# Local attention of a two-layer mixture kernel cut into units of 32 queries by 128 keys, with the turned probabilities as the stationary side of P V

## The chip, the cores and the metric

The kernel runs on one core of a Trainium2 chip, as one launch. The metric is the time of the device for one execution, in microseconds (us). The core has a matrix engine (TensorE, PE in the rows; its weight loads are PEld), VectorE (DVE), ScalarE (ACT), GpSimd (POOL) and SyncE (SP), which here only issues transfers (DMA).

## The reference, cut to what matters

```python
B, H, Sl, Sg, D = 4, 8, 512, 32, 64
k_all, v_all = concat([k_g, k_l]), concat([v_g, v_l])
out_g = sm(scale * q_g @ k_all.T) @ v_all                  # 32 global queries see all 544 keys
mask = abs(pos[:, None] - pos[None, :]) <= 32              # a local query sees 65 neighbours ...
s_ll = where(mask, scale * q_l @ k_l.T, -1e9)
out_l = sm(concat([scale * q_l @ k_g.T, s_ll])) @ v_all    # ... and the 32 global keys
x = concat([out_g, out_l], axis=2)                         # 4 x 544 = 2176 tokens of 512
h = x @ w_in ; x = (h * clip(h + 3, 0, 6) / 6) @ w_out     # 512 -> 2048 -> 512
out = max(x @ w1, x @ w2, x @ w3) @ w_out2                 # 512 -> 768 -> 512
```

`sm` takes the exponential of the row less its maximum and divides by the sum of the row plus 1e-9.

## The kernel before

**Stages.** Attention goes by batch b (4) and pair of heads pr (4 pairs), 16 pairs in all; the two heads of a pair lie in the two halves of the 128 partitions. Its result X, split into two fp32r parts, feeds the first product (`first`): 960 matmuls, 576 of 512 columns (token chunks 0 to 2) and 384 of 320 columns (chunks 3 and 4). Behind it come the second product in seven Strassen products (line 837), the third in seven (961), and the last (961, 1116).

**What sets the order.** Every step is an `op` with an engine, an estimated time and a due time; `Plan.order` puts the steps of each engine into one fixed order when the kernel is built. At run time each engine goes through its own list in that order and waits where a step is not ready. Attention steps are due by `STEPS` (s0 of a pair); `first` has a late due time (1e4 and more), so it fills PE's list where attention leaves room. SP issues nearly all transfers from one list.

**A pair before.** Keys are laid out as global, 256 local, global, 256 local, global (608 columns), so that 128 queries find their keys in a window of 224 columns. `scores` (L449) makes 16 matmuls of 64 queries by 128 to 192 keys with the two heads side by side. `rowmax` (L463, DVE) adds the mask and takes the maximum, `expo` (L469, ACT) the exponential and the sum, `guard` and `recip` (L480 to L485) make one over the sum, `norm` (L494, POOL) multiplies P by it. `flip` (L506) turns P by 16 transposes, four copies (`flipped`, L410) take it out of PSUM, and `pv` (L532) multiplies with V (64 columns) as the stationary side and turned P as the moving side, which leaves the result with the head's 64 values down the partitions, as X wants it (`x_hi` L547, `x_lo` L549).

**Global queries** go for two pairs at a time (`globals_`): `g_scores` (L566), `g_rowmax` (L570), `g_exp` (L578), `g_norm` (L583), five transposes (`g_flip`, L592), `g_pv` (L607), `g_x` (L611).

**Weights of the first product** (16 loads `raw`, 512 KB each) are decoded by DVE, ACT and POOL (L620 to L647) in the same stretch; after `first`, relu and gate (L683, L685) and the sums for Strassen (L655) follow, and the results go to DRAM (`gsA`, `gsB`, `gsC`).

**PSUM.** Five banks `s`, one bank `o` and two banks 6 and 7 serve attention and `first` until `end_of_attention`. There are three buffers each for Q, K and V.

Of the kernel before, what the change touches and what calls it, by code (L numbers as in the profile page):

```python
# [34 lines left out]
KEYS = {(0, 0): (0, 128), (0, 64): (0, 192), (1, 0): (0, 192), (1, 64): (64, 224),  # L35
        (2, 0): (0, 160), (2, 64): (32, 224), (3, 0): (32, 224), (3, 64): (96, 224)}
LOCAL = (((32, 192, 0),), ((0, 160, 96), (192, 32, 256)), ((0, 32, 224), (64, 160, 256)), ((0, 192, 320),))
SEEN = ((((0, 128), (0, 128)), ((1, 96), (64, 128))), (((0, 128), (0, 128)), ((1, 96), (0, 128))),
        (((0, 128), (0, 128)), ((1, 96), (32, 128))), (((1, 96), (0, 128)), ((0, 128), (0, 96))))
# [207 lines left out]
PAIRS = 3  # L247
SPLIT = 2
WIDE = 4
TS = "BC"  # L250
STEPS = (7.2, 13, 13, 15)
LAG = 92.0
# [12 lines left out]
def body(ctx, tc, q_n, k_n, v_r, w_in, w_o, w_3, w_4, out):  # L265
# [65 lines left out]
    mask_t = att.tile([128, 4, WIN], BF16, name="mask", bufs=1)  # L331
    nothing = att.tile([128, 288], BF16, name="nothing", bufs=1)
    mask = [Buf(tile=mask_t[:, 2 * u:2 * u + 2]) for u in range(2)]
    for u in range(2):
        nc.gpsimd.memset(mask_t[:, 2 * u:2 * u + 2], 0.0)
        for i in (2 * u, 2 * u + 1):
            for a, n, k0 in LOCAL[i]:

                far = 128 * i - k0
                for base, step in ((32 - far, 1), (32 + far, -1)):  # L340
                    if base + min(-step * 127, 0) + min(step * (n - 1), 0) < 0:
                        nc.gpsimd.affine_select(
                            out=mask_t[:, i, a:a + n], in_=mask_t[:, i, a:a + n], compare_op=ALU.is_ge, fill=-2.0 ** 33,
                            base=base, pattern=[[step, n]], channel_multiplier=-step)
# [10 lines left out]
    NTB = 8  # L355
    tbufs = []
    for i in range(NTB):
        t = att.tile([128, 2, 256], F32, name=f"tbuf{i}", bufs=1)
        nc.vector.memset(t[:, :, WIN:256], 0.0)
        tbufs.append(t)  # L360
    tg_t = att.tile([128, 640], F32, name="tg", bufs=1)
    nc.vector.memset(tg_t[:, 288:320], 0.0)
    nc.vector.memset(tg_t[:, NK:640], 0.0)
# [12 lines left out]
    T["vr"] = tag("vr", 3, [128, 2, 5, D], F32, "att")  # L376
    T["t"] = Tag("t", NTB, lambda slot: tbufs[slot], "att")
    T["tg"] = Tag("tg", 1, lambda slot: tg_t, "att")
    T["nm"] = tag("nm", 4, [128, 3, 2, 2], F32, "att")
    T["pt"] = tag("pt", 6, [128, 512], F32, "att")  # L380
    T["g1"] = tag("g1", 2, [128, 4], F32, "att")
# [34 lines left out]
    def pair(b, pr, s0):  # L416

        S = {}
        held[b, pr] = S
        Q, K, V = Buf(T["qr"]), Buf(T["kr"]), Buf(T["vr"])  # L420
        S["Q"], S["K"], S["V"] = Q, K, V

        for n, (t, src, cut, size) in enumerate(((Q, q_n, 256, NQ + SG), (K, k_n, 352, NK))):
            for i, (a, z) in enumerate(((0, cut), (cut, size)) if b + pr == 0 else ((0, size),)):
                e, issue = ("ACT", nc.scalar) if b + pr == 0 and n else ("SP", nc.sync)
                op(e, 0.45, lambda t=t, src=src, a=a, z=z, issue=issue: issue.dma_start(
                    out=t()[:, a:z], in_=src[b, pr][:, a:z]), s0 - 6 + i, w=[(t, i)] if b + pr == 0 else [t],
                   kb=(z - a) / 2, rel=s0 - 14, what="qk"[n])
        op("SP", 0.5, lambda: nc.sync.dma_start(out=V(), in_=v_r[b, pr]), s0 - 3 + 5 * (b + pr == 0), w=[V], kb=320, rel=s0 - 10, what="v")

        ob, PTS = Buf(T["o"]), {}

        for grp in (((0, 1),) if b >= PAIRS else ((0,), (1,))):
            SB, TB, NM, PT, FB = {}, {}, {}, {}, {}
            k, s1 = len(grp), s0 + 2 * grp[0]
            for u in grp:
                SB[u], TB[u] = ([Buf(T[x]) for _ in range(2)] for x in ("l" if b == 0 and u and pr < WIDE else "s", "t"))
                NM[u] = Buf(T["nm"])

            def scores(grp=grp, SB=SB):  # L440

                for u in grp:
                    for v in range(2):
                        i = 2 * u + v
                        for m in (0, 64):
                            for hh in range(2):
                                o, bank = 64 * hh, SB[u][hh]
                                a, z = KEYS[i, m]
                                nc.tensor.matmul(bank()[m:m + 64, v * WIN + a:v * WIN + z],  # L449
                                                 lhsT=Q()[o:o + 64, 128 * i + m:128 * i + m + 64],  # L450
                                                 rhs=K()[o:o + 64, 128 * i + a:128 * i + z], start=True, stop=True)

            need = [(Q, grp[0]), *((K, u) for u in range(grp[0] + 1))] if len(grp) == 1 else [Q, K]
            head = op("PE", 0.62 * k, scores, s1, r=need, after=full if b + pr == 0 else (),
               w=[x for u in grp for x in SB[u]] + [(t, "held") for u in grp for t in TB[u]], what="scores")
            if not full[6:]:
                full.append(filled(sbanks[4], [head]))
            for u in grp:
                sb, tb, nm = SB[u], TB[u], NM[u]
                for v in range(2):  # L460
                    for hh in range(2):
                        def rowmax(v=v, hh=hh, i=2 * u + v, sb=sb, tb=tb, nm=nm):
                            nc.vector.tensor_tensor_reduce(  # L463
                                out=tb[hh]()[:, v, 0:WIN], in0=sb[hh]()[:, v * WIN:v * WIN + WIN], in1=mask[i // 2]()[:, i % 2],
                                scale=-0.125, scalar=3.0e38, op0=ALU.add, op1=ALU.min, accum_out=nm()[:, 0, hh, v:v + 1])

                        def expo(v=v, hh=hh, tb=tb, nm=nm):
                            t = tb[hh]()[:, v, 0:WIN]
                            nc.scalar.activation(out=t, in_=t, func=ACTF.Exp, scale=-1.0, bias=nm()[:, 0, hh, v:v + 1],  # L469
                                                 accum_out=nm()[:, 1, hh, v:v + 1])  # L470

                        op("DVE", 0.47, rowmax, s0 + 2 * u + 1 + .2 * v, r=[(sb[hh], v), mask[u]],
                           w=[(tb[hh], v), (nm, (0, v, hh))], what="rowmax")
                        op("ACT", 0.665, expo, s0 + 2 * u + 2.2 + .2 * v, r=[(nm, (0, v, hh))],
                           w=[(tb[hh], v), (nm, (1, v, hh))], what="exp")

                def guard(e, nm=nm):
                    s = nm()[:, 1].rearrange("p h v -> p (h v)")
                    if e == "ACT":
                        nc.scalar.activation(out=s, in_=s, func=ACTF.Identity, bias=tiny)  # L480
                    else:
                        nc.gpsimd.tensor_tensor(out=s, in0=s, in1=tiny.to_broadcast([128, 4]), op=ALU.add)

                def recip(nm=nm):
                    nc.vector.reciprocal(out=nm()[:, 2], in_=nm()[:, 1])  # L485

                sums = [(nm, (1, v, hh)) for v in range(2) for hh in range(2)]
                op(("ACT", "POOL"), (0.295, 0.12), guard, s0 + 2 * u + 3, w=sums, what="guard", two=("POOL",))
                op("DVE", 0.175, recip, s0 + 2 * u + 3.5, r=sums, w=[(nm, 2)], what="recip")
                for hh in range(2):  # L490
                    def norm(hh=hh, tb=tb, nm=nm):
                        t = tb[hh]()[:, :, 0:WIN]
                        r = nm()[:, 2, hh].rearrange("p (v o) -> p v o", o=1).to_broadcast([128, 2, WIN])
                        nc.gpsimd.tensor_tensor(out=t, in0=t, in1=r, op=ALU.mult)  # L494

                    op("POOL", 0.98, norm, s0 + 2 * u + 4, r=[(nm, 2)], w=[(tb[hh], 0), (tb[hh], 1)], what="norm", two=True)
            for u in grp:
                FB[u], PT[u] = ([Buf(T[x]) for _ in range(2)] for x in ("f", "pt"))

            def flip(grp=grp, TB=TB, FB=FB):  # L500
                for u in grp:
                    for hh in range(2):
                        for v in range(2):
# [15 lines left out]
            if ONCE <= b < PAIRS:  # L519
                if not grp[0]:  # L520
                    continue
                grp, k = (0, 1), 2
# [682 lines left out]
```

## Time and profile before

| | |
|---|---|
| median of 3 runs | 733.1 us (731.78 to 734.84) |
| profiled execution, span | 729.2 us |
| the profiled execution's own time beside its span | not listed apart; the median lies 3.9 us over the span |
| PE busy | 717.7 us (98%) |
| DVE, ACT, POOL busy | 535.3, 411.0, 189.8 us |
| moved by DMA | 131.34 MB, mean 180 GB/s |

Busy time of PE counts matmuls that overlap in its pipeline, so it is not the time that the work needs; for that the chain of work that ended last is read, where each group of matmuls has the time from its start to the start of the next group.

### The profile page before, as it was taken

How to read it: one execution, taken by the hardware profiler on the slowest of the kernel's cores; microseconds unless marked ns; L12 is line 12 of the kernel's file. 1: busy time of each engine (PE TensorE's matmuls, PEld its weight loads, DVE VectorE, ACT ScalarE, POOL GpSimd, SP SyncE). 2: the span in 40 equal slices, each digit the busy share in tenths (PEclk: the TensorE clock that was granted, in tenths of full speed). 3: DMA queues.
4: the chain of work that ended last, by engine and by line, in shares of the span. 5: the costliest groups of instructions: out<-in, count | busy, mean ns of one | idle time of the engine just before them, and what ended most of it. 6: DMA issues, size and time to landing. Idle time of an engine off the chain costs nothing.

```text
span 729.2 us, 14100 instructions
## 1 busy us (share of the span) xinstructions
PE 717.7 (98%) x5329; PEld 638.1 (88%) x5329; DVE 535.3 (73%) x1100; ACT 411.0 (56%) x858; POOL 189.8 (26%) x225
## 2 busy tenths in 40 slices
PE   8999999999999999999999999999999999999998
PEld 6777878788888899988898899898999999998998
DVE  6979676546777766589976768999877886485881
ACT  7997889555544444356663457673644334253552
POOL 6685869322203122111000001121210220011210
PEclk9999999999999999999999999999999999999999
DMA  7455775424368884676565669401453562355652
GB/s 279 129 180 193 253 256 192 153 72 165 140 209 295 317 307 171 233 260 195 174 206 156 202 196 312 127 2 32 133 172 134 173 228 69 102 170 198 175 159 88
DMA packets 73140, 131.34 MB, mean 180 GB/s; under 512 B 4976, under 2 KB 43632, under 8 KB 72048
## 3 DMA queue, kind: packets, MB, share of 16 engines
q1 hardware_dynamic: 72784, 130.13, 53.6%
q8 instruction: 42, 0.69, 0.4%
q10 hardware_dynamic: 288, 0.31, 0.1%
q14 instruction: 26, 0.21, 0.1%
HBM read 84.93 MB, written 45.48 MB: 179 GB/s over the span
## 4 chain that ended last, share of the span: by engine, by line
PE 79%; DMA 6%; DVE 5%; ACT 4%; POOL 3%; issue 2%; SPq 0%; ACTq 0%; DVEq 0%; POOLq 0%
PE bank L961 31%; PE bank L673 21%; PE bank L837 20%; PE s L506 2%; ACT tbuf L469 2%; POOL rq L655 2%; PE o L532 2%; PE s L449 1%; DMA raw<-in_w_in_dram 1%; DMA gsA<-rq 1%; DMA kr<-in_kn_dram 1%; PE bank L1116 1%; POOL tbuf L494 1%; DVE rr L655 1%; PE s L607 1%
## 5 line engine op out<-in xcount | busy, mean ns | idle before, releaser
L673 PE MATMUL bank<-rx,rw 128*128 128x512 f32 (+1 forms) x960 | 199.1, 363 | 1.1 <-DVE rq L685 1.1
L673 PEld LDWEIGHTS bank<-rx,rw 128*128 128x128 f32 x960 | 161.2, 188 | 26.8 <-issue 4.3
L837 PE MATMUL bank<-rr,rw 128*128 128x320 f32 (+2 forms) x912 | 155.1, 331 | 1.0 <-DVE rr L655 0.9
L837 PEld LDWEIGHTS bank<-rr,rw 128*128 128x128 f32 x912 | 140.2, 188 | 15.0 <-DVE rr L655 1.9
L961 PE MATMUL bank<-rw,rr 128*128 128x256 f32 (+2 forms) x648 | 99.7, 302 | 1.1 <-DVE rf L973 0.7
L961 PEld LDWEIGHTS bank<-rw,rr 128*128 128x128 f32 x648 | 90.6, 188 | 6.1 <-DVE rf L973 1.1
L760 ACT CAST rr<-fw 128x1024 fp32r<-128x1024 f32 (+2 forms) x76 | 62.1, 820 | 52.3 <-PE bank L837 40.5
L655 DVE TENSOR_TENSOR rr<-fw,rr 128x1024 fp32r<-128x1024 f32 (+2 forms) x76 | 71.7, 947 | 25.1 <-ACT rr L760 24.4
L655 POOL TENSOR_TENSOR rf<-rf 128x256 f32<-128x256 f32 (+2 forms) x35 | 37.5, 1080 | 157.2 <-DVE rf L655 58.8
L469 ACT ACTIVATE tbuf<-tbuf,nm 128x224 f32<-128x224 f32 x128 | 60.6, 479 | 11.0 <-DVE nm L463 10.9
L685 DVE SCALAR_TENSOR_TENSOR rq<-rq,bank 128x512 f32<-128x512 f32 (+1 forms) x60 | 37.1, 619 | 38.4 <-ACT rq L683 38.1
L494 POOL TENSOR_TENSOR tbuf<-tbuf,nm 128x448 f32<-128x448 f32 x64 | 61.0, 973 | 8.4 <-DVE nm L485 4.9
L683 ACT ACTIVATE rq<-bank,three 128x512 f32<-128x512 f32 (+1 forms) x60 | 37.9, 632 | 43.5 <-PE bank L673 40.3
L410 ACT COPY rf<-bank 128x512 f32<-128x512 f32 (+2 forms) x72 | 33.2, 468 | 39.9 <-PE bank L961 29.5
L961 PE MATMUL bank<-rw,re 128*128 128x256 f32 (+2 forms) x369 | 54.2, 292 | 0.7 <-DVE bank L410 0.7
L961 PE MATMUL bank<-re,rr 128*128 128x512 f32 x222 | 54.8, 391 | 0.0
L655 POOL TENSOR_TENSOR rq<-rq 128x256 f32<-128x256 f32 (+2 forms) x45 | 38.5, 861 | 54.1 <-DVE rq L655 49.5
L961 PEld LDWEIGHTS bank<-rw,re 128*128 128x128 f32 x369 | 49.4, 188 | 2.4 <-DVE bank L410 0.9
L961 PEld LDWEIGHTS bank<-re,rr 128*128 128x128 f32 x222 | 40.8, 188 | 8.1
L1055 DVE TENSOR_TENSOR rf<-rf,bank 128x320 f32<-128x320 f32 (+2 forms) x72 | 37.0, 528 | 13.0 <-PE bank L961 11.7
L463 DVE CUSTOM_DVE_ANT_0 tbuf<-s,mask 128x224 f32<-128x224 f32 x112 | 36.9, 383 | 6.7 <-PE s L449 6.4
L506 PE MATMUL s<-ident,tbuf 128*128 128x128 f32 x256 | 33.9, 276 | 0.4 <-POOL tbuf L494 0.2
(131 smaller groups left out, 1047.4 us busy)
## 6 DMA issues: line engine op xcount, KB each, us to landing
fw<-gsB SPq DMA_DIRECT2D x28, 512.0 KB, 4.8
raw<-in_w_dram SPq DMA_DIRECT2D x24, 512.0 KB, 4.3
fw<-gsC SPq DMA_DIRECT2D x28, 320.0 KB, 3.6
raw<-in_w_in_dram SPq DMA_DIRECT2D x16, 512.0 KB, 4.0
raw<-in_w_o_dram SPq DMA_DIRECT2D x16, 512.0 KB, 4.9
fw<-gsA SPq DMA_DIRECT2D x28, 256.0 KB, 2.8
gsB<-rq SPq DMA_DIRECT2D x6, 1024.0 KB, 5.1
rf<-hd SPq DMA_DIRECT2D x14, 384.0 KB, 4.9
```

The source lines that it names most:

```text
L463: nc.vector.tensor_tensor_reduce(out=tb[hh]()[:, v, 0:WIN], in0=sb[hh]()[:, v * WIN:v * WIN + WIN], in1=mask[i // 2]()[:, i % 2], scale=-0 ...
L469: nc.scalar.activation(out=t, in_=t, func=ACTF.Exp, scale=-1.0, bias=nm()[:, 0, hh, v:v + 1], accum_out=nm()[:, 1, hh, v:v + 1])
L494: nc.gpsimd.tensor_tensor(out=t, in0=t, in1=r, op=ALU.mult)
L506: nc.tensor.transpose(FB[u][hh]()[:, at:at + 128], TB[u][hh]()[:, v, kb * 128:kb * 128 + 128], ident)
L655: ENG[e].tensor_tensor(out=out, in0=a, in1=b, op=f)
L673: nc.tensor.matmul(ps()[:, 0:m], lhsT=w[:, i, k], rhs=xs(c)[:, j, k], start=(k == 0 and s == 0), stop=(k == KC - 1 and s == 2))
L683: op("ACT", us, lambda ps=ps, m=m, out=out: nc.scalar.activation(out=out(), in_=ps()[:, 0:m], func=ACTF.Relu, bias=three), -100, r=[ps], w ...
L685: op("DVE", us, lambda ps=ps, m=m, out=out: nc.vector.scalar_tensor_tensor(out=out(), in0=out(), scalar=6.0, in1=ps()[:, 0:m], op0=ALU.min ...
L760: op("ACT", act(n) + 0.01, lambda: nc.scalar.copy(out=out(0), in_=src()), due, r=r, w=[(w, "hi")], what=what + "_hi")
L837: nc.tensor.matmul(A[e]()[:, 0:n], lhsT=w[:, 2 * fp + f, u, e], rhs=r[:, v, f], start=(seed is None and fp + f + s == 0), stop=(fp == 3 an ...
L961: nc.tensor.matmul(bank()[:, 0:n], lhsT=w[:, u, k], rhs=r[:, v, k], start=(start and k + s == 0), stop=(k == K - 1 and s == 2), skip_group ...
L1055: op("DVE", dve(n), lambda q=q, src=src, mv=mv: nc.vector.tensor_tensor(out=mv(q)(), in0=mv(q)(), in1=src(), op=ALU.max), -200, r=[bank], ...
```

## The change

A pair is now cut into 16 units of 32 queries with one window of 128 keys each: the keys are laid out as global, 64 local, global, 64 local, ... (800 columns), and a copy of V in windows of 128 rows is made on the host for each unit (2048 columns in place of 640). `scores` makes 32 matmuls of 32 queries by 128 keys, `rowmax` and `expo` work on 128 columns in place of 224, `flip` makes 8 transposes, and P is not normalized. `pv` has turned P (32 queries) as the stationary side and V (64 columns) as the moving side; its result has the queries down the partitions, is multiplied by one over the sums (`norm`, DVE, 512 columns) and turned by 4 transposes (`xflip`). The global queries follow the same manner. `STEPS` and `LAG` have other values, and the host function lays out K and V.

```diff
-STEPS = (7.2, 13, 13, 15)
-LAG = 92.0
+STEPS = (5.6, 9, 9, 10)
+LAG = 114.0
...
-FORM = dict(scores="Q", pv="H", g_scores="H", g_pv="H")
+FORM = dict(scores="Q", pv="R", g_scores="H", g_pv="R")
...
-    T["vr"] = tag("vr", 3, [128, 2, 5, D], F32, "att")
+    T["vr"] = tag("vr", 3, [128, 2, NW, D], F32, "att")
...
+        op("SP", 0.5, lambda: nc.sync.dma_start(out=V(), in_=v_r[b, pr]), s0 - 3 + 5 * first_, w=[V], kb=1024, rel=s0 - 10, what="v")
...
+                for i in tiles:
+                    for c in range(4):
+                        j = 4 * i + c
+                        a, z = SG * (j == 0), 128 - SG * (j == NW - 1)
+                        for hh in range(2):
+                            nc.tensor.matmul(SB[hh]()[QB * c:QB * c + QB, 128 * i + a:128 * i + z],
+                                             lhsT=Q()[64 * hh:64 * hh + 64, QB * j:QB * j + QB],
+                                             rhs=K()[64 * hh:64 * hh + 64, AT[j] + a:AT[j] + z], start=True, stop=True,
+                                             tile_position=(64 * hh, QB * c))
...
-                    def norm(hh=hh, tb=tb, nm=nm):
-                        t = tb[hh]()[:, :, 0:WIN]
-                        r = nm()[:, 2, hh].rearrange("p (v o) -> p v o", o=1).to_broadcast([128, 2, WIN])
-                        nc.gpsimd.tensor_tensor(out=t, in0=t, in1=r, op=ALU.mult)
...
+            def flip(hh=hh, FB=FB):
+                for i in range(4):
+                    nc.tensor.transpose(FB()[:, 128 * i:128 * i + 128], TB[hh]()[:, i], ident)
...
+            for i in range(4):
                 for hh in range(2):
+                    at = 128 * i + D * hh
+                    for c in range(4):
+                        nc.tensor.matmul(OB()[QB * c:QB * c + QB, at:at + D], lhsT=PT[hh]()[:, 128 * i + QB * c:128 * i + QB * c + QB],
+                                         rhs=V()[:, hh, 4 * i + c], start=True, stop=True, tile_position=(0, QB * c))
...
+        def norm():
+            r = NM()[:, 2].rearrange("p i h -> p (i h)").rearrange("p (x o) -> p x o", o=1).to_broadcast([128, 8, D])
+            nc.vector.tensor_tensor(out=OX().rearrange("p (x d) -> p x d", d=D), in0=OB().rearrange("p (x d) -> p x d", d=D),
+                                    in1=r, op=ALU.mult)
...
+        def xflip():
+            for i in range(4):
+                nc.tensor.transpose(XT()[:, 128 * i:128 * i + 128], OX()[:, 128 * i:128 * i + 128], ident)
...
+            for c, (j, k) in enumerate(GCHUNK):
+                for n, Z in enumerate(R):
                     for hh in range(2):
+                        x = 64 * n + 32 * hh
+                        at = 128 * (c % 4) + x
+                        nc.tensor.matmul(og()[x:x + 32, 0:D], lhsT=pts_g[c // 4]()[0:k, at:at + 32], rhs=Z["V"]()[0:k, hh, j],
+                                         start=(c == 0), stop=(c == 5), tile_position=(0, x))
```

The change moves instructions. On SP, at the start of the program, the list of transfers of before reads as follows (`qr`, `kr` and `vr` are the buffers of Q, K and V, `raw` that of encoded weights; the figures are partitions by elements).

```order
L426 DMA qr<-in_qn_dram 128x576
L426 DMA kr<-in_kn_dram 128x608
L429 DMA vr<-in_v_dram 128x640 x2
L426 DMA qr<-in_qn_dram 128x576
L426 DMA kr<-in_kn_dram 128x608
L642 DMA raw<-in_w_in_dram 128x4x256
L429 DMA vr<-in_v_dram 128x640
L642 DMA raw<-in_w_in_dram 128x4x256
```

At the same place the list of the change reads:

```order
L418 DMA qr<-in_qn_dram 128x576
L418 DMA kr<-in_kn_dram 128x800
L421 DMA vr<-in_v_dram 128x2048 x2
L418 DMA qr<-in_qn_dram 128x576
L418 DMA kr<-in_kn_dram 128x800
L421 DMA vr<-in_v_dram 128x2048
L418 DMA qr<-in_qn_dram 128x576
L418 DMA kr<-in_kn_dram 128x800
L630 DMA raw<-in_w_in_dram 128x4x256 x2
L418 DMA qr<-in_qn_dram 128x576
L418 DMA kr<-in_kn_dram 128x800
L421 DMA vr<-in_v_dram 128x2048 x2
```

The first encoded weights now stand behind three loads of V and the fourth pair's Q and K. Further down, the last load of V stands behind all 16 stores to `gsA` in the list of the change, and ahead of the first store to `gsB`:

```order
L687 DMA gsA<-rq 128x768
L687 DMA gsA<-rq 128x1024 x2
L421 DMA vr<-in_v_dram 128x2048
L740 DMA raw<-in_w_o_dram 128x1024 x4
L687 DMA gsB<-rq 128x1536
```

Before, three stores to `gsB` stood ahead of that load, too, so the last pair's attention has moved forward against the first product.

On PE, in the second batch, the steps of a pair of before stand like this, with `first` (L673) between them (`tbuf` holds P, `pt` turned P, `o` the result; scores are left out, since each is a row of its own).

```order
L506 MATMUL s_163<-ident,tbuf_146 128x128 x4
L506 MATMUL s_164<-ident,tbuf_148 128x128 x4
L592 MATMUL s_165<-ident,tg 128x128 x4
L592 MATMUL s_166<-ident,tg 128x128
L673 MATMUL bank_134<-rx,rw 128x512 x3
L566 MATMUL s_162<-kr,qr 64x288 x2
L607 MATMUL s_163<-pt,vr 64x32 x20
L532 MATMUL o<-pt,vr 64x128 x2
L532 MATMUL o<-pt,vr 64x64 x2
L532 MATMUL o<-pt,vr 64x128 x6
```

The same steps of the change, in its second batch (`t` holds P, `ox` the result before it is turned, `gx` that of the global queries):

```order
L489 MATMUL o<-vr,pt 32x64 x32
L586 MATMUL s_141<-vr,pt 32x64 x24
L542 MATMUL s_142<-kr,qr 64x192 x4
L542 MATMUL s_143<-kr,qr 64x160 x2
L594 MATMUL s_144<-ident,gx 128x128
L504 MATMUL s_140<-ident,ox 128x128 x4
L478 MATMUL s_141<-ident,t 128x128 x4
L661 MATMUL bank_129<-rx,rw 128x512 x12
```

`pv` has become 32 matmuls of 32 stationary columns, and transposes of the result stand behind it. Up to the last step of attention PE's list held 372 of the 960 matmuls of `first` before, and holds 234 now; 82 changes between shapes of the array before, 74 now.

## Rows read from the trace of the kernel before

**Rows 1.** The page: busy time by engine, and the chain by engine.
```profile
PE 717.7 (98%) x5329; PEld 638.1 (88%) x5329; DVE 535.3 (73%) x1100; ACT 411.0 (56%) x858; POOL 189.8 (26%) x225
PE 79%; DMA 6%; DVE 5%; ACT 4%; POOL 3%; issue 2%; SPq 0%; ACTq 0%; DVEq 0%; POOLq 0%
```

**Rows 2.** Windows: stretch (us), length, busy times, PEclk, DMA share, GB/s.
```profile
0.00:31.00 31.00, 28.02 (x385) 21.57 (x385) 24.21 (x114) 25.85 (x90) 20.90 (x40) 1.00 0.59 204
31.00:120.00 89.00, 87.45 (x902) 69.43 (x898) 66.80 (x218) 79.49 (x218) 66.31 (x79) 1.00 0.64 220
120.00:206.00 86.00, 84.92 (x840) 70.22 (x837) 49.56 (x156) 50.43 (x145) 27.21 (x41) 1.00 0.38 136
206.00:306.00 100.00, 100.00 (x580) 92.52 (x579) 67.93 (x118) 41.95 (x73) 22.39 (x21) 1.00 0.73 261
306.00:729.00 423.00, 417.30 (x2636) 384.40 (x2635) 326.84 (x500) 213.29 (x335) 53.02 (x47) 1.00 0.51 160
...
100.00:120.00 20.00, 20.00 (x239) 16.18 (x239) 14.25 (x62) 19.72 (x59) 17.52 (x23) 1.00 0.81 290
240.00:260.00 20.00, 20.00 (x116) 18.36 (x115) 14.82 (x26) 7.58 (x13) 1.41 (x1) 1.00 0.96 339
```

**Rows 3.** The chain that ended last, at the start: start (us), length, engine, line.
```profile
5.95 4.29 ACT tbuf L469 x18
...
25.51 0.30 DVE tbuf L463
...
31.17 0.90 PE bank L673 x3
```

**Rows 4.** The same chain, 146 to 306 us.
```profile
146.30 1.75 PE s L506 x16
...
150.01 1.70 PE o L532 x32
151.71 1.14 PE s L607 x40
152.84 0.94 PE s L566 x8
153.79 0.90 PE bank L673 x3
154.69 1.30 PE s L449 x32
...
203.06 102.80 PE bank L673 x588
...
269.93 10.12 PE bank L673 x69
```

**Rows 5.** The timeline of PE from 134.79 to 134.82 us: start, length, line.
```profile
134.79 0.39 PE L449 MATMUL s<-kr,qr 64*64 64x128 f32 x4
```

**Rows 6.** Groups by line and shape: busy us, mean ns; idle before.
```profile
L469 ACT ACTIVATE tbuf<-tbuf,nm 128x224 f32<-128x224 f32 x128 | 60.6, 479 | 11.0 <-DVE nm L463 10.9
L410 ACT COPY pt<-s 128x512 f32<-128x512 f32 x52 | 28.2, 581 | 4.9 <-PE s L506 2.9 <-PE s L592 1.6 <-ACT pt L410 0.2
L578 ACT ACTIVATE tg<-tg,g 128x576 f32<-128x576 f32 x8 | 6.2, 778 | 4.7 <-DVE g L570 4.6
L463 DVE CUSTOM_DVE_ANT_0 tbuf<-s,mask 128x224 f32<-128x224 f32 x112 | 36.9, 383 | 6.7 <-PE s L449 6.4 <-issue 0.3
L570 DVE CUSTOM_DVE_ANT_0 tg<-s,nothing 128x288 f32<-128x288 f32 x8 | 3.6, 448 | 3.0 <-PE s L566 3.0
L549 DVE TENSOR_TENSOR rx<-o,rx 128x512 fp32r<-128x512 f32 x12 | 8.2, 687 | 4.2 <-ACT rx L547 4.0
L494 POOL TENSOR_TENSOR tbuf<-tbuf,nm 128x448 f32<-128x448 f32 x64 | 61.0, 973 | 8.4 <-DVE nm L485 4.9 <-ACT tbuf L469 3.5
```

**Rows 7.** Transfers by line: KB each, us from issue to landing.
```profile
vr<-in_v_dram SPq DMA_DIRECT2D x16, 320.0 KB, 5.3
kr<-in_kn_dram SPq DMA_DIRECT2D x15, 304.0 KB, 5.4
```

**Rows 8.** Waits of SP's list: line, released by, us in total, times, longest.
```profile
SPq L429 <- PE s L607: 21.0, 9, 14.4
```

More of the change, by code (lines that the diff above doesn't have):

```diff
@@ L431, in pair @@
[L431 to L455, printed above, removed]
@@ new lines, in pair, with scores @@
+        op("SP", 0.5, lambda: nc.sync.dma_start(out=V(), in_=v_r[b, pr]), s0 - 3 + 5 * first_, w=[V], kb=1024, rel=s0 - 10, what="v")
+        TB, NM, OB = [Buf(T["t"]) for _ in range(2)], Buf(T["nm"]), Buf(T["o"])
+        for u, tiles in enumerate(((0, 1), (2, 3)) if first_ else (range(4),)):
+            SB = [Buf(T["l" if b == 0 and (u or pr == 2) else "s"]) for _ in range(2)]
+            k, s1 = len(tiles) / 4, s0 + u
+            def scores(tiles=tiles, SB=SB):
+                for i in tiles:
[7 more added lines that the diff above has]
+                                             tile_position=(64 * hh, QB * c))
+            need = [(Q, u), *((K, x) for x in range(u + 1))] if first_ else [Q, K]
+            head = op("PE", 0.1 + 0.86 * k, scores, s1, r=need, after=full if first_ else (),
+                      w=SB + [(t, "held") for t in TB], what="scores")
@@ L509, in pair @@
-            op("PE", 0.1 + 0.87 * k, flip, s1 + 5, r=[(TB[u][hh], v) for u in grp for hh in range(2) for v in range(2)],
-               w=[x for u in grp for x in FB[u]] + [Buf(T["turn"])], what="flip")
-            for u in grp:
-                for hh in range(2):
-                    e = AD if b == 0 else "DVE" if hh and u else "ACT"
-                    us = (0.585, 0.65)
-                    op(e, us if b == 0 else us[e == "DVE"], lambda e=e, pt=PT[u][hh], fb=FB[u][hh]: copy(e, pt(), fb()),
-                       s0 + 2 * u + 6, r=[FB[u][hh]], w=[PT[u][hh]], what="flipped")
@@ new lines, in guard @@
+        def guard(e):
+            s = NM()[:, 1].rearrange("p i h -> p (i h)")
+            if e == "ACT":
+                nc.scalar.activation(out=s, in_=s, func=ACTF.Identity, bias=tiny)
+            else:
+                nc.gpsimd.tensor_tensor(out=s, in0=s, in1=tiny.to_broadcast([128, 8]), op=ALU.add)
+        sums = [(NM, (1, i, hh)) for i in range(4) for hh in range(2)]
+        op(("ACT", "POOL"), (0.295, 0.12), guard, s0 + 5, w=sums, what="guard", two=("POOL",))
+        op("DVE", 0.18, lambda: nc.vector.reciprocal(out=NM()[:, 2], in_=NM()[:, 1]), s0 + 5.5, r=sums, w=[(NM, 2)], what="recip")
@@ L538, in pair @@
+        op("PE", 0.48, xflip, s0 + 9, r=[OX], w=[XT], what="xflip")
         for c, (t0, n) in enumerate(CHUNKS):
@@ L561, in globals_ @@
+        for a, ks in enumerate((GKEYS[0:2], GKEYS[2:3])):
             sg = Buf(T["s"])
[L563 to L572 removed]
@@ new lines, in globals_ @@
+        op("ACT", 1.04, lambda: nc.scalar.activation(out=tg()[:, 0:672], in_=tg()[:, 0:672], func=ACTF.Exp, scale=-1.0,
+                                                     bias=g1()[:, 2:3], accum_out=g1()[:, 3:4]), g0 + 2, w=[g1, tg], what="g_exp")
+        op("POOL", 0.12, lambda: nc.gpsimd.tensor_tensor(out=g1()[:, 3:4], in0=g1()[:, 3:4], in1=tiny, op=ALU.add),
+           g0 + 3, w=[g1], what="g_guard", two=True)
+        op("DVE", 0.2, lambda: nc.vector.reciprocal(out=g1()[:, 4:5], in_=g1()[:, 3:4]), g0 + 4, w=[g1], what="g_recip")
@@ new lines, in globals_ @@
+        op("PE", 0.72, g_pv, g0 + 8, r=pts_g + [Z["V"] for Z in R], w=[og], what="g_pv")
+        gx, xt = Buf(T["gx"]), Buf(T["s"])
+        op("DVE", 0.3, lambda: nc.vector.tensor_scalar(
+            out=gx(), in0=og()[:, 0:D].rearrange("p (o d) -> p o d", o=1).to_broadcast([128, 2, D]), scalar1=g1()[:, 4:5], scalar2=None,
+            op0=ALU.mult), g0 + 9, r=[og, g1], w=[gx], what="g_norm")
+        op("PE", 0.15, lambda: nc.tensor.transpose(xt()[:, 0:128], gx().rearrange("p o d -> p (o d)"), ident), g0 + 9.5, r=[gx], w=[xt],
+           what="g_turn")
@@ L614, in join @@
+        for hh in range(2):
+            op("ACT", 0.24, lambda hh=hh: nc.scalar.copy(
+                out=xG()[64 * hh:64 * hh + 64, pr - 1:pr + 1, b],
+                in_=xt()[64 * hh:64 * hh + 64, 0:128].rearrange("p (n h q) -> p n h q", n=2, h=2)[:, :, hh]), g0 + 10, r=[xt],
+               w=[(xG, (b, pr, hh))], what="g_x")
     def join(part, t, r, key, due):
```

232 lines of the change are left out of this document (94 added, 138 removed).

## The prediction

> **What bounds the kernel now.** I read the page first: PE is busy for 98% of the span and holds 79% of the chain that ended last [rows 1]. Then the windows by stage [rows 2], to see where PE waits. The reader should see that the last 423 us hold 417 us of PE work, and that the stretch of the attention (0 to 206 us) has PE nearly full too, but with all the others loaded beside it: ACT 25.85 of 31 us at the start and 79.49 of 89 us behind it. At the very start it is ACT, not PE, that leads: the chain goes through nine exponentials and their sums in 4.29 us and later through DVE's maxima, and only at 31.17 us comes the first matmul of `first` [rows 3]. The granted clock is 1.00 in all stretches of rows 2, so it plays no part in the sum.
>
> The sum is made on the chain [rows 4], since busy time counts overlap twice. It prices each group by the time until the next one starts. A pair costs 1.30 (scores) + 1.75 (16 transposes) + 1.70 (`pv`) = 4.75 us. A global step costs 1.14 (`g_pv`) + 0.94 (`g_scores`) + five transposes at 1.75/16 = 0.109, 0.55, so 2.63 us. 16 pairs and 8 global steps: 97.0 us. `first`: the 320-column matmul takes 10.12/69 = 0.147 us; of the 588 from 203.06 us 384 are such, 56.4 us, which leaves 46.4 us for 204 of 512 columns, 0.227 us each. All of `first` is 576 x 0.227 + 56.4 = 187.2 us. It ends at 203.06 + 102.80 = 305.9 us. With some 3 us of fill matmuls at the start, 305.9 - 97.0 - 187.2 - 3 = 18.7 us of the first stage are waits and changes of shape.
>
> **The change part by part, PE first.** The trace has only larger tiles than the new ones, so I look for the rule in the rows. Each matmul on f32 leaves two records: the 16 of a pair's scores are 32 [rows 4]. Transposes cost 0.109 us for 128 columns, 0.85 ns a column. The scores are 8 groups of four (two heads, two halves of queries) whose widest member has 192 columns: 1.30/8 = 0.163 us, again 0.85 ns a column. So matmuls on different parts of the array share one pass. `g_pv` with 32 columns doesn't follow: 40 records in 1.14 us, pairs every 0.057 us, where 0.85 ns would give 0.027. That is either the loading of 2 x 64 stationary columns or a floor of 0.0285 us per matmul.
>
> - Scores, 64 records a pair in groups of eight with 128 columns: 8 x 0.109 = 0.87 us at best, 64 x 0.0285 = 1.82 us if each matmul costs what one of `g_pv` does. I take 0.95, with a change of shape.
> - `pv`, 64 records in groups of four with 4 x 32 stationary and 64 moving columns: 16 x 0.057 = 0.91 us by the same loading of 128 columns, 1.82 us by the floor. I take 1.05: the old one, by its columns (2 x 896 x 0.85 ns = 1.52), shows 0.18 us for the change of shape as well.
> - 8 transposes in place of 16, 0.87 us; `xflip` adds four, 0.44 us.
>
> A pair is then 3.31 us. A global step: scores of 544 columns twice at 0.85 ns, 0.92; six transposes 0.65; `g_pv` 12 x 0.057 = 0.68; one more transpose 0.11: 2.36 us. Together 16 x 3.31 + 8 x 2.36 = 71.8 us in place of 97.0: **PE is relieved of 25 us**. I take the low ends because four matmuls of the scores, in four parts of the array, start within 0.03 us [rows 5], which speaks against a fixed price for each; the high ends stay in the range. Changes of shape fall from 82 to 74 at some 0.1 us (three matmuls of `first` between two such changes take 0.90 us, against 0.68), 0.8 us, not counted.
>
> The Trainium skill speaks against this change: "TensorE: Matmul & The Clock Gate", in the section on why a gap is 56 and not 53.3 ns, says that the distance from start to start never falls below about 25 ns however few columns move. The mean of 28.5 ns in `g_pv` agrees with it, the four starts in 30 ns do not. It has a rival of its own below.
>
> **The others.** Exponentials of 128 columns: ACT's slope is (778 - 479)/(576 - 224) = 0.85 ns a column [rows 6], so 128 x 82 ns = 10.5 us less. ACT copied turned P 52 times at 0.581 us and does so 22 times, 17 us less. POOL loses 64 `norm` at 0.973 us, 61 us. DVE loses 128 x 0.10 us on the maxima (slope (448 - 383)/64 = 1 ns) and gains 16 `norm` at about 0.69 us (a 512-column operation on PSUM [rows 6]), so a few us less. None of this is on PE's path after 31 us, so I give it nothing, but a pair's time on ACT falls by about 1.7 us, which is what lets pairs follow each other faster at the start.
>
> DMA is where the change pays. K grows from 304 to 400 KB and V from 320 [rows 7] to 1024 KB a pair: 16 x 800 KB = 13.1 MB more. The highest rate is 339 GB/s at a share of 0.96 [rows 2], so 353 GB/s when nothing rests. Up to the last load of V SP's list issues Q and K (16 x 688 KB), V (16 x 1024), 18 weight loads (512 each) and the stores to `gsA` (7168 KB): 43,776 KB, 44.8 MB, **127 us at 353 GB/s**. PE's list holds until the end of attention 71.8 + 3 + 234 x 0.227 = 128 us. So transfers and PE are now equal, where before the same stretch ran at shares of 0.59, 0.64 and 0.38 [rows 2]. PE's order is fixed: if V is late PE waits at `pv`, though later parts of `first` could run. V loads also wait for a buffer until `g_pv` is through (21.0 us in all before [rows 8]), and weights, Q and K queue behind them on SP; three times the bytes come after each such wait.
>
> How full will the queues be? The best 20 us of this stage had 0.81, the best of the run 0.96 [rows 2]; I take 0.885, the middle: 127/0.885 = 143.5 us until the last V has landed. Behind it stand that pair's `pv`, the global step and nine matmuls of `first`, with a landing of some 2 us: 8 us. Then 726 of `first`: 342 x 0.227 + 56.4 = 134.0 us. `first` ends at 285.5 us, against 305.9: **20.4 us earlier**. At a share of 1 it is 269, which is below PE's own 262 + waits of 9 us at the start, so 271 us; at 0.81 it is 299.
>
> What follows `first` is moved forward as it is: PE's groups there have the same counts and order. `LAG` shifts only when weights are asked for. That is priced at nothing since 417.3 of 423 us are PE work there; without that cover the 5.7 us of waits could change by as much either way.
>
> Span 729.2 - 20.4 = 708.8; the median lay 3.9 us above this span (733.1), so **713 us**.
>
> **Rivals.**
> 1. *The transfers hold attention back further* (share 0.81 or below, or ACT and DVE, which carry the same weight decoding in less time). `first` then ends at 299 us or later: 726 us at 0.81, 733 at 0.775. For it: no 20 us of the first 206 us went above 0.81. Against: before, nothing asked for more.
> 2. *Each small matmul costs as much as one of `g_pv`* (28.5 ns). A pair is 1.82 + 1.82 + 1.31 = 4.95, a global step 0.92 + 0.65 + 1.37 + 0.11 = 3.05, together 103.6 us: 6.6 us more than before, **740 us, slower**. It decides from 25.8 ns a matmul: 16 x (128 p + 1.31) + 8 x (48 p + 1.68) = 97.0. For it: 28.5 ns is the least mean in the trace. Against: rows 5.
> 3. *A floor of 25 ns for each start.* PE's part is 95.2 us, 1.8 us less: 731 us, no change. This is the skill's rule named above.
> 4. *The gain is given back after `first`*, by weights or stores that come at another time: 729 to 735 us.
>
> **How the numbers follow.** The forecast has 0.60, its own range 699 to 724 (shares 1 to 0.82). Rival 1 has 0.18, two thirds of it faster; rival 2 0.10; rival 3 0.06; rival 4 0.06. A change of 0.5%, 3.7 us, is about what a measurement of this kernel can tell from none. Faster: 0.60 + 0.12 + 0.02 = 0.74; slower: 0.10 + 0.02 = 0.12; the same: 0.14. The range 700 to 731 takes the forecast, nearly all of rival 1 and rival 3.
>
> **What would show it.** Right: scores near 0.9 and `pv` near 1 us on the chain, transposes at 0.109, the last `g_pv` at 145 to 155 us in place of 203, `first` through at 280 to 290, a DMA share of 0.85 or more over the first 140 us, and PE waits for `vr`, `kr` or `raw`. Wrong: 64 records in 1.6 us or more (rivals 2, 3); attention that ends after 165 us with PE waiting for DMA, ACT or DVE (rival 1); a distance from the end of `first` to the end of the span other than 423 us (rival 4).

## The result, and the profile after

The changed kernel takes **723.7 us** (median of 5, 723.41 to 727.77) against 733.25 us (median of 5) of before: ratio 0.988, 95% interval 0.986 to 0.991. That is a gain of 9.6 us where 20 were forecast; the range of 700 to 731 us holds it. The profiled execution is the slowest of the five (727.77 us, span 726.0); the other spans run down to 721.6 us.

The page after: busy time, the granted clock in 40 slices, PE's instruction queue (packets, MB, share), the chain by engine. They answer to [rows 1].

```profile
PE 701.8 (97%) x6401; PEld 624.1 (86%) x6401; DVE 528.2 (73%) x1110; ACT 382.3 (53%) x813; POOL 126.3 (17%) x162
...
PEclk9799999999999999999999999999999999999999
...
q8 instruction: 50, 0.82, 0.5%
...
PE 87%; DMA 5%; DVE 4%; ACT 2%; issue 2%; SPq 0%; POOL 0%; ACTq 0%; DVEq 0%
```

The windows by stage, as in [rows 2], and two shorter ones:

```profile
0.00:31.00 31.00, 23.34 (x602) 17.95 (x603) 16.51 (x94) 18.07 (x69) 4.48 (x23) 0.89 0.83 311
31.00:120.00 89.00, 81.64 (x1693) 64.66 (x1691) 73.04 (x275) 72.45 (x237) 35.26 (x50) 0.94 0.85 300
120.00:206.00 86.00, 84.50 (x956) 69.22 (x945) 59.33 (x157) 44.60 (x115) 16.62 (x24) 1.00 0.63 226
206.00:306.00 100.00, 100.00 (x593) 92.71 (x592) 56.51 (x99) 35.26 (x63) 21.77 (x20) 1.00 0.62 226
306.00:726.00 420.00, 412.34 (x2582) 379.55 (x2580) 322.79 (x491) 211.94 (x333) 48.20 (x45) 1.00 0.50 158
...
20.00:40.00 20.00, 15.96 (x358) 12.73 (x362) 12.75 (x67) 14.07 (x53) 1.81 (x4) 0.68 0.57 207
80.00:100.00 20.00, 19.38 (x484) 15.78 (x486) 17.24 (x64) 17.29 (x54) 11.22 (x16) 1.00 1.00 351
```

DMA comes near what was forecast: a share of 0.83 to 0.85 over the first 120 us, and 1.00 at 351 GB/s at its best. But PE, which was busy for 28.02 of the first 31 us [rows 2], is so for 23.34, and the clock is no longer 1.00. The chain shows where PE stands still ("issue" is time in which it waits for nothing that the profile shows):

```profile
26.88 0.66 PE s L478 x4
27.53 1.01 PE s L435 x55
28.55 1.05 PE o L489 x64
29.60 1.07 PE s L542 x12
30.67 0.37 PE s L435 x15
31.04 2.67 issue
33.71 1.54 PE s L435 x43
...
60.30 1.01 PE s L435 x55
...
76.86 0.44 PE s L478 x4
...
92.67 1.03 PE o L489 x64
...
99.69 0.67 PE s L586 x48
100.36 2.81 issue
```

And the waits of PE (line, releaser, us in all, times, longest):

```profile
PE s L435 <- issue: 5.5, 2, 2.8
PE bank L435 <- issue: 3.6, 1, 3.6
...
PE o L489 <- issue: 1.4, 2, 0.8
...
PE s L435 <- DMA kr<-in_kn_dram: 0.9, 2, 0.7
...
PE o L489 <- DMA vr<-in_v_dram: 0.4, 1, 0.4
```

The reader should see that the groups themselves cost what was forecast (`pv` 1.03, four transposes 0.44 us; of a pair's 64 score records 55 stand on the chain with 1.01 us, and from the first of all 64 to the next group it is 1.03, 51.60 to 52.63 us in the last two rows below), that K and V make PE wait 1.3 us in all, and that 10.5 us are stops inside or ahead of `scores` and `pv` with no releaser. Four of these five stops lie between two matmuls of one group, as at 17.07 us:

```profile
15.39 1.10 PE L489 MATMUL o<-vr,pt 128*32 128x64 f32 x64
16.42 0.65 PE L435 MATMUL bank<-kr,qr 64*32 64x96 f32 x28
20.69 1.38 PE L435 MATMUL bank<-kr,qr 64*32 64x128 f32 x36 [3.62 <-issue]
...
51.60 1.10 PE L435 MATMUL s<-kr,qr 64*32 64x96 f32 x64
52.63 0.97 PE L661 MATMUL bank<-rx,rw 128*128 128x512 f32 x3
```

The last matmul of `first` starts at 299.2 us (before: 305.6), the last step of attention at 163.2 (202.8).

**What ends the stops.** Queue q8 of the page brings instructions: 50 packets of 16.4 KB for 12,856 records of PE (matmuls and weight loads, and a few waits), 42 for 10,735 before, so I take it that they are PE's, 256 instructions a packet (50 x 256 = 12,800, 42 x 256 = 10,752), 64 bytes each. Counting PE's records from 0, the five stops stand in front of numbers 449, 705, 1217, 3265 and 4033, all of the form 256 k - 63. During each of the three long ones, one q8 packet lands (18.09 to 19.23, 31.16 to 32.11, 100.64 to 101.73 us), and PE goes on some 1.5 us behind it (20.69, 33.71, 103.18). The Trainium skill ("Trainium Architecture — The Big Picture", section on the software stack) has instructions of 64 bytes, which agrees, and has the streams moved to the engines when the program is loaded; here PE's stream comes in pieces while the program runs. In the first 310 us the time lost in front of exactly such numbers is 12.1 us, against 0 before (from the start of one record to the start of the next, where that is over 0.3 us).

### The profile page after: what moved, and what is told of

It is laid out like the page before. It is cut to its first block, busy times and chain, and to the rows that moved or that the text cites. A ratio compares the mean times of both kernels' runs of the same rounds, so it can differ in the third digit from the quotient of the medians.

```text
span 726.0 us, 16109 instructions
## 1 busy us (share of the span) xinstructions
PE 701.8 (97%) x6401; PEld 624.1 (86%) x6401; DVE 528.2 (73%) x1110; ACT 382.3 (53%) x813; POOL 126.3 (17%) x162
## 4 chain that ended last, share of the span: by engine, by line
PE 87%; DMA 5%; DVE 4%; ACT 2%; issue 2%; SPq 0%; POOL 0%; ACTq 0%; DVEq 0%
PE bank L949 31%; PE bank L661 23%; PE bank L825 22%; PE o L489 2%; PE s L435 2%; PE s L478 2%; ACT t L454 1%; PE bank L1104 1%; DMA gsB<-rq 1%; DMA vr<-in_v_dram 1%; DMA raw<-in_w_in_dram 1%; PE s L504 1%; PE s L542 1%; DMA out_dram<-rf 1%; DMA raw<-in_w_o_dram 1%
## 5 line engine op out<-in xcount | busy, mean ns | idle before, releaser
L673 DVE SCALAR_TENSOR_TENSOR rq<-rq,bank 128x512 f32<-128x512 f32 (+1 forms) x60 | 37.0, 619 | 36.8 <-ACT rq L671 36.5
L643 POOL TENSOR_TENSOR rf<-rf 128x256 f32<-128x256 f32 (+2 forms) x34 | 33.4, 989 | 164.1 <-DVE rf L643 43.4
L454 ACT ACTIVATE t<-t,nm 128x128 f32<-128x128 f32 x128 | 49.8, 392 | 12.4 <-DVE nm L448 12.1
L401 ACT COPY rf<-bank 128x320 f32<-128x320 f32 (+2 forms) x72 | 33.1, 467 | 41.9 <-PE bank L949 33.4
L448 DVE CUSTOM_DVE_ANT_0 t<-s,mask 128x128 f32<-128x128 f32 x116 | 27.3, 283 | 13.5 <-PE s L435 13.4
L643 DVE TENSOR_TENSOR rf<-rf 128x256 f32<-128x256 f32 (+4 forms) x54 | 30.4, 597 | 7.0 <-DMA rf<-hd 6.9
L643 DVE TENSOR_TENSOR re<-rf,re 128x1024 fp32r<-128x1024 f32 (+4 forms) x20 | 26.0, 1307 | 3.9 <-ACT re L1126 3.9
```

Source lines behind the costliest of these rows:

```text
L401: (nc.scalar.copy if eng == "ACT" else nc.vector.tensor_copy)(out=out, in_=in_)
L448: nc.vector.tensor_tensor_reduce(out=TB[hh]()[:, i], in0=SB[hh]()[:, 128 * i:128 * i + 128], in1=mask()[:, (i + 1) // 2 if i < 3 else 2], ...
L643: ENG[e].tensor_tensor(out=out, in0=a, in1=b, op=f)
L673: op("DVE", us, lambda ps=ps, m=m, out=out: nc.vector.scalar_tensor_tensor(out=out(), in0=out(), scalar=6.0, in1=ps()[:, 0:m], op0=ALU.min ...
```

## The experiments

**Theory F:** PE runs out of its own instructions; `scores` and `pv` use up 128 in about 1 us, and the packets with new ones come late through full queues. **Rivals:** the added bytes make data late (D); the other `STEPS` and `LAG` do it. "Stops" below is this time lost in front of numbers 256 k - 63 in the first 310 us (the expectations have 12.8 us for the change and 0.5 for before, by a wider count), "first" the start of its last matmul, "rest" the time from there to the end of the span.

**1. The bytes: `e1_no_late_v`, `e2_before_more_bytes`.** The change without the V of pairs 3 to 15, and the kernel before with 10.5 MB more.

```diff
+            if n_pair < 3:
+                nc.sync.dma_start(out=V(), in_=v_r[b, pr])
+            else:
+                V.tile = vs[n_pair % 3]()
```

> The changed kernel without the transfers of V for pairs 3 to 15 (they multiply by the V of pairs 0 to 2, so that part of the result is not computed), same orders on all engines, 13.6 MB less. Theory F (PE stops because its own instructions, which come through the same queues in pieces of 256, are late; 10.5 us of stops inside groups of matmuls in the changed kernel, and a lower clock behind them): the stops inside groups at 31 and 100 us vanish, the granted clock is 1.00 from 40 us on, the first product ends at 285 to 290 us instead of 299, the time is 711 to 716 us. Theory D (K, V and weights land late, and PE waits for them by semaphore): such waits of PE were only about 2 us, so 720 to 722 us, and stops inside groups stay.

713.42 us, ratio 0.975 (0.971 to 0.978); first 287.9, stops 6.6: F's numbers met, D's missed. Those at 31 and 100 us fall to nothing and 0.65 us, the one in front of number 705 stays (3.9 us on the profile's list).

```diff
+            for x in junk:
+                nc.sync.dma_start(out=x, in_=v_r[b, pr])
```

> The kernel before with two more transfers of 320 KB beside each load of V, from DRAM to DRAM, whose result nobody reads (10.5 MB more, most of what the change adds). Theory F: the kernel before needs 256 instructions of PE only every 9 us or so, half as often as the change does at its densest, so stops inside groups are below 2 us in all and the time rises by 0 to 4 us (733 to 737). Theory D, by which the bytes alone cost what is missing: 740 us or more, with PE waiting for K, V or weights.

745.29 us, ratio 1.019 (1.016 to 1.023): F's numbers missed, D's met. 10.5 MB more cost before 13 us (732.34 us beside it), 13.6 MB less bring the change 10 us, but by another way: before has no stop with them, and PE's longest wait there is for K:

```profile
PE s L456 <- DMA kr<-in_kn_dram: 6.4, 4, 3.4
```

So full queues take part, and these two runs can't tell F from D.

**2. The place of the stops: `e5_shift`.** 32 more fill matmuls ahead of everything.

```diff
-        for j in range(4):
+        for j in range(4 + 32 * (bank is sbanks[0])):
+            j = j % 4
```

> The changed kernel with 32 more fill matmuls (64 instructions of PE) ahead of the first scores, while PE has nothing to do; all else is the same. Theory of the instruction supply: PE stops when the pieces of 256 instructions that have been fetched are used up, so the long stops without a semaphore stand again in front of PE's instructions number 449, 705, 1217 or another 256 k - 63, which are now 64 instructions earlier in the work (a different matmul of the group, or another group). Lengths may differ, since other packets are under way; median 719 to 728 us. Rival, that something at these places of the work makes PE wait (a tile, a transfer, a change of shape): the stops stay in front of the same matmuls of the work, now numbers 513, 769, 1281; median 722 to 726.

724.35 us. The timeline of PE at the stop in front of number 705, to be set beside that of the change above:

```profile
16.96 1.09 PE L490 MATMUL o<-vr,pt 128*32 128x64 f32 x60
19.52 0.30 PE L490 MATMUL o<-vr,pt 128*32 128x64 f32 x4 [1.46 <-issue]
19.75 0.47 PE L436 MATMUL bank<-kr,qr 64*32 64x96 f32 x18
```

It has moved from behind the 28th record of `scores` to behind the 60th of 64 of `pv`: 28 + 4 matmuls with their weight loads are 64 instructions, to the last one. The stop in front of 1217 moved in the same way (3.41 us, behind the 60th record of a `pv`). No data and no tile is special at these places: it is the count.

**3. The count of instructions: `e11_half_the_instructions`, `e12_before_twice`.**

```diff
-                    for c in range(4):
+                    for c in (0, 2):
...
-   SB[hh]()[QB * c:QB * c + QB, ...], lhsT=Q()[..., QB * j:QB * j + QB]
+   SB[hh]()[QB * c:QB * c + 64, ...], lhsT=Q()[..., QB * j:QB * j + 64]
```

(`pv` likewise.)

> The changed kernel with scores and pv on 64 queries at a time and the keys and values of the first 32 (the windows of every second unit are thus not computed): half as many matmuls, each of the same columns, two in place of four side by side. PE's time by columns is the same (8 groups of 128 and 8 of 64 columns), all transfers too; 128 instructions a pair fewer, some 2000 of 12,856. If what PE lacks is instructions, used up at 128 per us in scores and pv: the stops in front of 256 k - 63 lose half or more of their 12.8 us, first is done at 288 to 293, median 712 to 718. If full queues alone set them: they stay at 10 us or more, first done at 297 to 301, median 721 to 727. If four matmuls side by side were worth more than the columns say, scores and pv get longer than 1.2 us and the kernel slower than 727.

**710.88 us**, ratio 0.970 (0.967 to 0.973); first 283.7, stops 0. The windows show the queues as full as ever and the clock at 1.00; the chain shows that the groups cost the same:

```profile
0.00:31.00 31.00, 25.27 (x440) 19.93 (x442) 21.61 (x121) 23.31 (x89) 5.99 (x25) 1.00 0.95 357
31.00:120.00 89.00, 88.74 (x1207) 70.83 (x1202) 75.88 (x282) 76.23 (x245) 40.37 (x55) 1.00 0.93 336
...
34.81 1.08 PE o L489 x32
...
36.70 1.03 PE s L435 x32
```

This is the run that decides: same bytes, same columns, half the matmuls of `scores` and `pv`, and 12.8 us come back.

The converse on before cuts each matmul of `scores` and `pv` in two by columns (`x` in `range(2)`, half of the columns each). Other than its expectation says, its sums in `pv` are not those of the reference; columns, transfers and counts of instructions are as meant.

> The kernel before with each matmul of scores and pv cut in two by its columns: the same result, the same columns and the same transfers, but 128 instructions of PE more for each pair, about as many in all as the change has. If the rate of PE's instructions alone makes it stop: stops in front of instructions 256 k - 63 come to 3 us or more (0.5 in before), first is done at 309 us or later, median 736 to 742. If it takes full queues as well, which this kernel doesn't have (share 0.6): the stops stay under 2 us, first is done at 305 to 308, median 732 to 736. If each half matmul costs more than half, scores and pv get longer than 1.30 and 1.70 us.

735.06 us, ratio 1.003 (1.002 to 1.005), stops 0.3, first 307.3. About as many instructions as the change has, spread over 204 us in place of 163 and with queues at a share of 0.6, cost hardly a stop. So the count in all isn't enough, and by the run before it full queues aren't either. That it takes both, a fast use and a late packet, is what the sum below says; no run here had the fast use with empty queues.

**How the two add up.** No packet of q8 in the profiled runs of before, of the change or of half the instructions starts before PE has come within 294 instructions of the place where it will run out. So I set the time that PE takes for these 294 (worked out from the records) beside the time until the packet lands:

| | PE's 294 instructions, us | packet lands after, us | stop, us |
|---|---|---|---|
| change, number 705 | 5.1 | 7.5 | 3.9 |
| change, 1217 | 3.3 | 4.6 | 2.9 |
| change, 4033 | 6.7 | 8.3 | 3.0 |
| half the instructions, the two latest packets | 13.0; 13.1 | 7.9; 7.6 | 0 |
| before twice, the latest | 13.5 | 7.6 | 0 |

Landing + 1.5 us - PE's time gives the stops: 3.9, 2.8, 3.1.

**4. V on its own queue, and nearly no V: `e10_v_on_pool`, `e9_no_v`.** `nc.gpsimd.dma_start` for V; V of the first pair alone.

> The changed kernel with its V loads issued from POOL in place of SP, so that they stand in a queue of their own and K, Q and the weights don't wait behind them; bytes and PE's instructions are unchanged. Theory of the instruction supply: the same bytes still stand ahead of PE's own packets, so the stops in front of instructions 256 k - 63 stay, 9 us or more in all, median 719 to 728. Rival, that the order of SP's one queue is what makes everything late: the stops and the waits for K shrink, first is done before 294, median 712 to 718.

730.94 us, ratio 0.996 (0.993 to 0.999); stops 10.4, at other numbers of the same form, and V and K late by 4.7 us each. The stops stay, as F said; the cost of a second queue it had not foreseen.

> The changed kernel, with V loaded for the first pair alone; all later pairs multiply by that V (so the part of the result that rests on the other V is not computed). Orders and instruction counts are those of the change. The run that loaded V for the first three pairs kept one stop of 4.16 us in front of PE's instruction 705 at 17.28 us, with first done at 287.9 us. If that stop comes of full queues: it falls under 1.5 us, first is done at 282 to 285, median 706 to 711. If it comes of the rate at which PE uses up instructions, full queues or not: it stays above 3 us, first done at 286 to 289, median 711 to 716.

711.01 us; first 286.1, stop in front of 705 3.13 us on the profile's list: the second theory's numbers. The queues were not empty there (share 0.84 from 15.5 to 20 us, K, Q and weights), so it doesn't show that the rate alone suffices.

**5. `STEPS` and `LAG`: `e3_steps_before`, `e4_steps_between`, `e6_between_lag_kept`, `e7_slow_start`, `e8_lag_before`.** Two lines each; what was set stands in the table.

> The changed kernel with STEPS and LAG of before, so that a pair starts every 13 us instead of every 9. Theory F: the same instructions and bytes over a longer stretch, share of the queues 0.5 to 0.65, no stop inside a group behind the first 35 us, 712 to 718 us. Theory D: about the same. A third theory, by which the denser attention is itself worth something to PE: 726 us or more.

> The changed kernel with STEPS (6.4, 11, 11, 12) and LAG 103, between the two. Theory F: one or two stops inside groups left behind 35 us, 714 to 720 us; between the changed kernel (723.7) and the one with the steps of before. If the pace has nothing to do with it: 722 to 725 us.

> The changed kernel with STEPS halfway (6.4, 11, 11, 12) and its own LAG of 114. The run of these STEPS with LAG 103 had first done at 295.2 us and then took 432.5 us more, 6 to 9 more than the change. If LAG alone loses the end: first is done at 294 to 297 and the rest takes 423 to 427 us, span 717 to 724, median 717 to 722. If the later transfers of these STEPS lose it, LAG or not: the rest again takes 430 or more, median 729 to 734.

> The changed kernel with STEPS (6.4, 9, 9, 10): only the pairs of the first quarter follow each other more slowly; LAG 114. Theory of the instruction supply: with less asked of the queues in the first 35 us, the stops at 17 and 31 us and the low clock behind them shrink by 3 us or more together; first is done at 291 to 297, median 714 to 721. Rival, that the instructions are late whenever scores and pv stand close together, full queues or not: the stops only move, first is done at 298 to 301, median 722 to 727.

> The changed kernel with LAG 92 as before, and the change's own STEPS. If LAG sets what the end costs: first is done at 298 to 300 as with the change, the rest takes 431 or more, median 729 to 734. If it doesn't: the rest takes 423 to 427, median 721 to 726.

| | STEPS, LAG | median, us | stops | first | rest |
|---|---|---|---|---|---|
| change | (5.6, 9, 9, 10), 114 | 723.68 | 12.1 | 299.2 | 426.8 |
| `e8` | same, 92 | 734.08 | 11.0 | 301.6 | 435.3 |
| `e3` | (7.2, 13, 13, 15), 92 | 731.22 | 4.3 | 296.8 | 434.2 |
| `e4` | (6.4, 11, 11, 12), 103 | 732.25 | 5.9 | 295.2 | 432.5 |
| `e6` | same, 114 | 725.04 | 10.6 | 299.7 | 424.6 |
| `e7` | (6.4, 9, 9, 10), 114 | 723.09 | 9.7 | 296.1 | 425.8 |

`LAG` is worth some 8 us behind `first` in the profiled runs (435.3 against 426.8, 432.5 against 424.6) and 10.4 and 7.2 us of the medians. At 92, in `e8`, products there wait up to 5.4 us at a time for a split on DVE, which stands behind the splits of late weights in DVE's list:

```profile
PE bank L825 <- DVE rr L643: 5.9, 2, 5.4
```

F's numbers for `e3` and `e4` missed, and not only because they left `LAG` out: without its 8 us the two would be at some 723 and 724 us (an estimate), still above 718 and 720. Their stops shrank to 4.3 and 5.9 us, but with pairs that start later `first` came only 2 to 4 us earlier. `STEPS` alone changes nothing that can be measured; in `e7` the stop in front of 705 stays (3.6 us), as its rival said, though `first` falls among F's numbers.

**6. Why the packet is late: `e13_v_in_four`, `e14_all_in_four`, `e15_v_by_columns`, `e16_and_weights`.** The Trainium skill ("DMA: Bandwidth & Descriptors", section on queues, rings and completion order) says that a DMA engine turns to its next queue only when it has drained a packet of the one it is at. If so, smaller transfers should let PE's packet through sooner.

```diff
+            for x in range(0, 128, 32):
+                nc.sync.dma_start(out=V()[x:x + 32], in_=v_r[b, pr][x:x + 32])
```

> The changed kernel with each V load issued as four transfers of 32 partitions (256 KB, 16 KB for each of 16 DMA engines, 0.73 us at 353 GB/s, in place of 64 KB and 2.9 us); same bytes, same lists otherwise. If PE's packet waits for the single transfer that a DMA engine is busy with: the stops at instructions 256 k - 63 that fall in V loads shrink, 12.8 us in all to 8 or less, first is done at 290 to 296, median 715 to 720. If it waits for all that was issued before it: stops stay at 10 to 14 us, median 721 to 727. If four issues on SP's list cost more than they bring, K and V come later and the waits for kr and vr rise above 3 us: 725 to 731.

> As the run with V in four, and Q, K (but for the first pair's) and the encoded weights of the first product in four transfers each as well. If size is the cause, the stop at 17 us in front of instruction 705, where K, Q and weights are under way and which stayed at 3.4 us without V, falls under 2 us too: stops 5 us or less in all, first done at 287 to 292, median 712 to 717. If all that was issued counts: stops 10 to 14 us, 721 to 727. If SP's issues bind: waits for kr and raw, 725 or more.

748.37 and 769.26 us: both theories missed, since pieces of 32 partitions are slower themselves. In the first stage of `e13` the DMA engines are busier than in the change (0.83) and move less (311 GB/s there):

```profile
0.00:31.00 31.00, 17.96 (x387) 13.71 (x388) 10.19 (x59) 9.89 (x38) 4.30 (x22) 0.81 0.96 244
```

Cut by columns (`V()[:, hh, x:x + 8]`, all 128 partitions), the rate is that of the change again, in the first stage and from 80 to 100 us:

```profile
0.00:31.00 31.00, 22.96 (x587) 17.73 (x587) 16.58 (x94) 18.26 (x69) 4.48 (x23) 0.89 0.89 308
...
80.00:100.00 20.00, 19.44 (x491) 15.88 (x491) 17.09 (x64) 17.48 (x54) 11.05 (x17) 1.00 1.01 347
```

> The changed kernel with each V load issued as four transfers of 128 partitions by 512 columns (256 KB each), in place of four by 32 partitions. First: windows at a share of 0.9 or more should again show 330 GB/s or more, else this cut is no test either. If PE's packet waits for the single transfer that a DMA engine is busy with: the stops at 256 k - 63 fall from 12.8 to 8 us or less, median 715 to 720. If it waits for all that was issued before it: stops 10 to 14 us, median 721 to 727.

> As the run before it, and the encoded weights of the first product in four transfers of 128 KB each too. If size is the cause, the stop at 17 us falls under 2 us and the stops come to 5 us or less, median 712 to 718. If all that was issued counts: stops 10 to 14 us, 721 to 727. If four issues each on SP's list bind: K and V late, waits for kr and vr over 3 us, 726 or more.

725.95 and 724.19 us. The stops in front of 705 and 1217 are halved (1.7 and 1.5 us, 1.6 and 1.5), and all stops together fall from 12.1 to 8.1 and 5.4 us, close to the numbers for size as the cause. But the times are those of its rivals: PE's waits that have a releaser grow over the first 300 us from 5.7 to 10.9 and 13.5 us, with 3.4 and 4.5 for K (0.9 with the change). So the size of a transfer seems to be part of it, but smaller ones bring no gain here; what else makes the packet land up to 8.3 us behind the point where 294 instructions are left stays open. No run that computes the whole result was measurably faster than the change.

## Why the prediction was right and wrong

**PE's relief: right.** A pair costs 1.03 + 1.03 + 0.88 + 0.44 = 3.38 us (forecast 3.31), a global step 1.07 + 0.66 + 0.67 + 0.26 = 2.66 (2.36). Together 75.4 in place of 97.0 us: 21.6 us of the 25.2. 64 records of `scores` or `pv` take 16 ns each, which refutes rivals 2 and 3; the floor of about 25 ns of the Trainium skill ("TensorE: Matmul & The Clock Gate", the section named in the prediction) does not hold here for matmuls that stand side by side in the array.

**DMA: right, once PE doesn't stand still.** Share 0.83 to 0.85 over 120 us (0.885 taken), at 0.93 to 0.95 with half the instructions. With those, the last V lands at 142.4 us (forecast 143.5), `first` starts its last matmul at 283.7 us (forecast for its end: 285.5) and the span is 709.1 (708.8). Rival 1 gave 726, near the result, but data is not what PE waited for.

**The step that failed** is "127/0.885 = 143.5 us until the last V has landed": it let the transfers alone set when V comes, and PE wait for data alone. The last V was issued at 152.23 us and landed 4.8 us later, at 157.1 us. What stands behind it, 8 + 134.0 = 142 us in the forecast, held: `first` ends at 299.5, 142.4 us later. Up to that V the queues had a share of 0.80, and its loads waited 19.5 us for PE to give a buffer free (10.3 us with half the instructions, at a share of 0.86):

```profile
152.23 0.33 SPq L421 DMA_DIRECT2D vr<-in_v_dram  x1
...
SPq L421 <- PE s L586: 19.5, 7, 9.1
```

By the sum itself a share of 0.80 gives 127/0.80 + 142 = 301 us. So it is luck that the range holds the result: it had a low share in it, but for full queues, not for a PE that lacks instructions.

By the working of the 18.7 us, `first` less its work and fills leaves 299.5 - 75.4 - 187.2 - 3 = 33.9 us of waits with the change and 284.0 - 265.6 = 18.4 with half the instructions (18.7 before). Of the 15.5 us between them, 12.1 are the stops for PE's own instructions, a cost that the sum had no term for. The rest, some 3 us, fits the clock, which "plays no part in the sum": from 20 to 40 us it was granted at 0.68, so partly at the lower of 1.2 and 2.4 GHz, behind PE's stop of 3.62 us; four transposes at 26.88 us take 0.66 in place of 0.44. That share was not tested by itself.

**Behind `first`:** `LAG` priced at nothing was right for the profile (420 us with 412 of PE), but only because the change raised it; with 92 the gain would be gone (`e8`). The 3 us that the profiled run loses there are one gap at 668.1 us, in the slowest execution; a run with the same lists but for its fills (`e5`) has a rest of 423.1. Rival 4 so has at most these 3 us, and no part in the median is shown.

## What to carry to other kernels

When a change cuts matmuls into smaller ones, count the instructions too, not only columns and bytes: at 64 bytes each they come through the same DMA engines, and by the table above PE's time for the last 294 of them must exceed the landing of the next packet by some 1.5 us; it landed after 4.6 to 8.3 us where PE stopped in the change. Stops with no releaser at even distances in the count of instructions are the sign; half as many matmuls of twice the stationary columns (in a run that left half of the windows out) took them away here; another pace, another queue or smaller loads only moved or lessened them. A parameter that shifts loads for a later stage deserves a price of its own, even where that stage's work doesn't change.

## What was unexpected of the hardware

- PE's instructions arrive in packets of 256 while the program runs. PE stops in front of number 256 k - 63 when one is late, and starts 1.3 to 1.6 us after it has landed.
- 32 matmuls of 32 stationary columns (64 records) take as long as 16 of 64: 1.03 against 1.08 us for `pv`, 1.03 against 1.03 for `scores`.
- With V in transfers of 32 partitions by 8 KB the first stage moved 244 GB/s at a share of 0.96; with the same bytes as 128 partitions by 2 KB it moved 308 at 0.89.
